# Filter taps on all partitions: a block transposition in place of fp32 matmuls in a convolution and ReGLU kernel

## The chip, the cores and the metric

The kernel runs on one core of one Trainium2 chip. The metric is the device time of one execution in microseconds (us); plain runs are timed without a profiler, and one more execution was profiled. TensorE is shown as PE (its weight loads as PEld), VectorE as DVE, ScalarE as ACT, GpSimd as POOL, SyncE as SP.

## What is computed

Eight sequences of 4096 tokens with 192 channels pass a causal convolution of seven taps and then a gated feed-forward layer. The taps are softmax weights, one set for each of eight heads of 24 channels.

```
w = weight - max(weight)              # weight: 8 heads x 7 taps
w = exp(w) / (sum(exp(w)) + 1e-9)
x_pad = 6 zero tokens ahead of x      # x: 8 x 4096 x 192
y[b, s, h, :] = sum over k of w[h, k] * x_pad[b, s + k, h, :]
out = (max(y @ w_gate, 0) * (y @ w_val)) @ w_out    # 192 -> 1536 -> 192
```

## The kernel before

The eight sequences are worked on in two streams of four, side by side: 64 rows of TensorE's array, and 64 channels of a third, belong to each stream. A unit is 1024 tokens of both streams; there are 16 units. For each unit and each half of 512 tokens, `gate_val` (L539) runs twelve column blocks of 128: six 64-row matmul pairs for gate and value (L552), a Relu on ACT (L563), a product on DVE (L564). `project` (L647) then multiplies by w_out (L581), copies out of PSUM (L607) and stores.

The convolution is done in two ways. For most of the kernel it is done off TensorE: POOL reads and rearranges x for a unit ahead (L203, L476), SP transposes it (L480), and ACT, DVE and POOL form the seven products and sums, with the taps as a scalar for each channel (`tap`, read at L496, L512, L526). The first unit can't wait for that. Its two blocks of 512 tokens are convolved on TensorE by `conv_dense` (L352): x stands as tokens by channels, and each head has a band matrix of 118 by 112 with its seven taps along the diagonals. Matmuls (L377) of 32 and fewer channels go to four column groups of the array, two for each stream.

The order of instructions on every engine is the order of the program text (the schedule is manual); the waits between engines are put in by the framework.

What is done ahead of the first convolution, with the names that matter:

- `wr` is the weight, 8 partitions by 7; it is loaded first on SP's queue (L101). Behind it on the same queue comes x of the first block, first stream, into a staging area in fp32 (L122), and the first 96 tokens of both streams (L138). The second stream comes through POOL's queue, cast on the way, into `x_h` (L127).
- `spaced` is a mask that POOL makes with a memset (L126) and an affine_select (L128). DVE sums it in two ways (`summed`, L238) to get `same` and `places`.
- DVE and ACT form the maximum (L251), the exponentials `ex`, each repeated 16 times (L254), the sum and its reciprocal (L258, L259). Two fp32 matmuls (L272, one instruction in the text) spread the taps from 8 partitions to 112. `diag` (L282) is taps times mask, and 14 matmuls (L292) build the bands in PSUM from `places` and `diag`; `fill_band` (L332) copies them to SBUF.
- `warm_up` (L154) gives TensorE matmuls whose result is not read: six and a half of 512 columns at the start, one behind L272, one behind L292.
- `taps` (L304) is the scaled taps on 8 partitions. Ten DMAs of SP (L310) spread them over `tap`, ahead of the first convolution; POOL copies `tap` to the other 64 partitions much later (L698).
- ACT casts the first stream's x in two pieces (L317), DVE the first tokens (L338).
- In `conv_dense`, for the first block and the first third of the channels, `both_halves` copies w_gate and w_val to the other 64 partitions (L177), and the matmuls run stream by stream:

```
        late = (1, 2, 3, 4, 0)
        both = [(jj, (0, 1)) for jj in late]
        if g == 0 and c == 0:
            both = [(jj, (st,)) for st in range(2) for jj in late[0:4]] + both[4:]
```

`first_block` (L387) does the three thirds and evicts each (L392) to `xc`, which L552 reads.

Of the kernel before, what the change touches and what calls it, by code (L numbers as in the profile page):

```python
# [7 lines left out]

FP = mybir.dt.float32
F16 = mybir.dt.float16  # L10
ACTF = mybir.ActivationFunctionType
ALU = mybir.AluOpType

# [2 lines left out]
def kernel(  # L16
# [12 lines left out]
    nc = tc.nc  # L29

    B, S, D = x.shape
    H, KW = weight.shape
    G = D // H
# [3 lines left out]
    NCH = D // 64  # L37
# [11 lines left out]
    UNIT = 2 * WIN  # L49
# [11 lines left out]
    const = ctx.enter_context(tc.tile_pool(name="const", bufs=1))  # L61
# [5 lines left out]
    xcpool = ctx.enter_context(tc.tile_pool(name="xcpool", bufs=3))  # L67
# [3 lines left out]
    psum = ctx.enter_context(tc.tile_pool(name="psum", bufs=4, space=bass.MemoryType.PSUM))  # L71
# [22 lines left out]

    xts = {}
    ROWS0 = DSUB + PAD
    GAP = 12
    SEG = 16
    NSEG = SUB // SEG
    wr = const.tile([H, KW], FP)  # L100
    nc.sync.dma_start(out=wr[:], in_=weight)  # L101
# [13 lines left out]
    def body(st):  # L115
# [4 lines left out]
        )  # L120

    nc.sync.dma_start(out=stage(0, SUB, 0, 1, 1, GSUB - 1), in_=body(0))  # L122
# [3 lines left out]
    nc.gpsimd.memset(spaced[:], 0.0)  # L126
    nc.gpsimd.dma_start(out=xts[0][0:SUB, 1:GSUB, 1, :], in_=body(1))  # L127
    nc.gpsimd.affine_select(  # L128
        out=spaced[:, :, GAP : GAP + SEG],
        in_=ones[0:SUB, 0 : KW * SEG].rearrange("p (k s) -> p k s", k=KW),  # L130
        pattern=[[-SEG, KW], [-1, SEG]],
        compare_op=ALU.is_equal,
        fill=0.0,
        base=0,
        channel_multiplier=1,
    )
    nc.vector.memset(stage(0, 32, 0, 2, 0, 1), 0.0)
    nc.sync.dma_start(  # L138
        out=stage(PAD, FIRST, 0, 2, 0, 1),
# [1 line left out]
            tensor=x.tensor, offset=x.offset, ap=[[D, FIRST], [NB * S * D, 2], [1, D]]  # L141
        ),
    )
    spare = const.tile([H, 1], FP)
    nc.scalar.activation(spare[:], ones[0:H, 0:1], ACTF.Exp)

    places = const.tile([SUB, 2 * SUB], F16)
    nc.vector.memset(places[:], 0.0)
# [3 lines left out]
    def warm_up(*widths):  # L152
        for n, w in enumerate(widths):
            nc.tensor.matmul(  # L154
                out=warm[:, n % 2, 0:w], lhsT=busy[:, 0:128], rhs=busy[:, 0:w], start=True, stop=True
            )

    warm_up(512, 512, 512, 512, 512, 512, 256)

# [69 lines left out]
    pool_halves(3)  # L229
    load_w(5, 2)  # L230

    ex = const.tile([H, KW + 1, SEG], FP)
    nc.vector.memset(ex[:], 1e-9)
    some = spaced[:, 0, 0:1]

    def summed(out, step, n, at):
        with nc.allow_low_precision("one of the terms is not zero"):
            nc.vector.tensor_reduce(  # L238
                out=out,
                in_=bass.AP(  # L240
                    tensor=some.tensor,
                    offset=some.offset + at,
                    ap=[some.ap[0], [1, n], [step, KW]],
                ),
                axis=mybir.AxisListType.X,
                op=ALU.add,
            )

    pitch_k = SEG + 2 * GAP
    mx = const.tile([H, 1], FP)  # L250
    nc.vector.tensor_reduce(  # L251
        out=mx[:], in_=wr[:], axis=mybir.AxisListType.X, op=ALU.max, negate=True
    )
    nc.scalar.activation(  # L254
        ex[:, 0:KW, :], wr[:].unsqueeze(2).to_broadcast([H, KW, SEG]), ACTF.Exp, bias=mx[:]
    )
    sm = const.tile([H, 1], FP)
    nc.vector.tensor_reduce(out=sm[:], in_=ex[:, :, 0], axis=mybir.AxisListType.X, op=ALU.add)  # L258
    nc.vector.reciprocal(sm[:], sm[:])  # L259
    over = const.tile([H, H], FP)  # L260
    nc.vector.tensor_scalar(
        out=over[:],
        in0=spaced[0:H, 0, GAP : GAP + H],
        scalar1=sm[:],
        scalar2=None,
        op0=ALU.mult,
    )
    same = const.tile([SUB, SEG], FP)
    summed(same[:], pitch_k, SEG, GAP)
    summed(places[:, SUB - SEG : SUB - SEG + SEG + KW - 1], pitch_k - 1, SEG + KW - 1, GAP)  # L270
    spread = psum.tile([128, 2, 512], FP, name="ps")
    nc.tensor.matmul(  # L272
        out=spread[0:SUB, 0, 0:H],
        lhsT=ex[:, 0:KW, :].rearrange("h k s -> h (k s)"),
        rhs=over[:],
        start=True,
        stop=True,
    )
    warm_up(512)
    diag = const.tile([SUB, H, SEG], F16)  # L280
    with nc.allow_low_precision("products with one and zero"):
        nc.vector.tensor_tensor(  # L282
            out=diag[:],
            in0=spread[0:SUB, 0, 0:H].unsqueeze(2).to_broadcast([SUB, H, SEG]),
            in1=same[:].unsqueeze(1).to_broadcast([SUB, H, SEG]),
            op=ALU.mult,
        )
    bps = psum.tile([128, 2, 512], FP, name="ps")
    HB = H // 2
    for a in range(2):  # L290
# [7 lines left out]
                skip_group_check=True,  # L298
            )

    warm_up(512)

    taps = const.tile([H, KW], FP)
    nc.scalar.activation(taps[:], ex[:, 0:KW, 0], ACTF.Copy, scale=sm[:])  # L304
    tap = const.tile([128, NCH, KW], FP)
    for h in range(H):
        r = G * h
        while r < G * (h + 1):
            c, n = r // 64, min(64 - r % 64, G * (h + 1) - r)
            nc.sync.dma_start(  # L310
                out=tap[r % 64 : r % 64 + n, c, :],
                in_=taps[h : h + 1, :].unsqueeze(1).to_broadcast([1, n, KW]),
            )
            r += n

    for cols in (slice(0, 64), slice(64, D)):
        nc.scalar.copy(  # L317
            out=xts[0][0:ROWS0, 1:GSUB, 0, cols],
            in_=stage(0, ROWS0, 0, 1, 1, GSUB - 1)[:, :, cols],
        )  # L320
    bands, wide_bands, ends = {}, {}, []

    def fill_band(a, heads, copy):
# [10 lines left out]
            in_=from_.rearrange("p (b h s) -> p h b s", h=HB, s=SEG)[:, lo : lo + n],  # L334
        )

    fill_band(0, [0, 1, 2], nc.vector.tensor_copy)
    nc.vector.tensor_copy(  # L338
        out=xts[0][0 : FIRST + PAD, 0, :, :], in_=stage(0, FIRST + PAD, 0, 2, 0, 1)
    )  # L340
    fill_band(0, [3], nc.vector.tensor_copy)
    fill_band(1, [4, 5], nc.scalar.copy)
    fill_band(1, [6, 7], nc.scalar.copy)

    def band(h):
# [2 lines left out]
    xc = {}  # L348
# [3 lines left out]
    def conv_dense(g, c, ps, bank):  # L352


        xt = xts[g]
        if g == 0 and c == 0:
            xc[0] = xcpool.tile([128, NCH, UNIT], F16, name="xc")
            both_halves(nc.vector.tensor_copy, 0, Wg)
            both_halves(nc.vector.tensor_copy, 0, Wv)
        toks = GROUPS[g][1]  # L360
        t0 = toks[0]
        ends = toks[1:] + [t0 + WIN]
        late = (1, 2, 3, 4, 0)
        both = [(jj, (0, 1)) for jj in late]
        if g == 0 and c == 0:
            both = [(jj, (st,)) for st in range(2) for jj in late[0:4]] + both[4:]
        for jj, sts in both:
            col, n = toks[jj] - t0, ends[jj] - toks[jj]
            rows = n + PAD
            for second in range(2):  # L370
                for st in sts:
                    for k2 in range(2):
                        k = 2 * c + k2
                        h0, h1 = 32 * k // G, (32 * k + 31) // G
                        h, m = (h0, G * h1 - 32 * k) if second else (h1, 32)
                        p0 = 64 * st + 32 * k2
                        nc.tensor.matmul(  # L377
                            out=ps[p0 : p0 + m, bank, col : col + n],
                            lhsT=xt[0:rows, jj, st, 32 * k : 32 * k + m],
                            rhs=band(h)[0:rows, 0:n],  # L380
                            start=True,
                            stop=True,
                            tile_position=(0, p0),
                            skip_group_check=True,
                        )

    def first_block():  # L387
        for c in range(NCH):
# [300 lines left out]


    first_block()
    both_halves(nc.vector.tensor_copy, 1, Wg)
    both_halves(nc.vector.tensor_copy, 1, Wv)
    pool_halves(4)
# [74 lines left out]
```

## Time and profile before

| | |
|---|---|
| plain runs | 765.69 us median of 3 (765.66 to 765.76) |
| the profiled execution | 767.53 us |
| its span, first to last instruction | 765.8 us |
| granted TensorE clock, mean of the span | 1.000 |
| busy PE, PEld | 762.0 us, 547.1 us |
| busy DVE, ACT, POOL | 705.9 us, 601.1 us, 378.9 us |

A row of the timeline gives start and length in us, the engine (with a q for its queue, where it issues a DMA), the line, the operation, the tile written and those read, shapes, how many instructions the row merges, and in brackets how long the engine was idle before it and what ended that. A row of the chain gives start, length, and what ran. A row of a table of windows gives the window, its length, and for each engine the busy time and the number of instructions that touch it; then the granted clock, the load of the DMA engines and GB/s. A row of DMA issues ends with the median time from issue to landing.

### The profile page before, as it was taken

Reading aid. Unit: us, or ns where it says so; the run is one execution under the profiler, and the core shown is the slowest. Engines: PE = TensorE matmul, PEld = TensorE weight load, DVE = VectorE, ACT = ScalarE, POOL = GpSimd, SP = SyncE. Lnnn points to the kernel's source line nnn. Section 1 sums busy time; section 2 is a strip of 40 time slices with the busy share of each in tenths; the row PEclk is TensorE's granted clock in tenths of the full one; section 3 lists DMA queues with packets and bytes.
Section 4 is the critical chain, followed back from the end, with each engine's and each line's share of the span. In section 5 each row is a group of like instructions: output and inputs, shape, how many; then the busy total and the mean of one; then the engine's idle time right before and its main releaser. Section 6 shows DMA issues by size and latency. Waiting matters only on the chain.

```text
span 765.8 us, 25125 instructions
## 1 busy us (share of the span) xinstructions
PE 762.0 (99%) x10937; PEld 547.1 (71%) x10937; DVE 705.9 (92%) x763; ACT 601.1 (78%) x735; POOL 378.9 (49%) x248
## 2 busy tenths in 40 slices
PE   9999999999999999999999999999999999999998
PEld 5496785957759577695866858668595775957758
DVE  6998999999999999999999999999999999999891
ACT  6787887878878787887878878788787887876571
POOL 8518549093570926719165290853908447090000
PEclk9999999999999999999999999999999999999999
DMA  9969138180362904529063281732818034110202
GB/s 121 125 111 138 18 95 82 53 117 11 99 79 66 114 23 99 56 85 94 23 109 50 85 93 44 110 25 89 89 44 130 8 96 61 65 49 13 73 1 84
DMA packets 131830, 56.00 MB, mean 73 GB/s; under 512 B 96392, under 2 KB 131720, under 8 KB 131720
## 3 DMA queue, kind: packets, MB, share of 16 engines
q1 hardware_dynamic: 90680, 38.81, 23.2%
q0 software_dynamic: 40896, 15.50, 20.3%
q8 instruction: 85, 1.39, 0.8%
q14 instruction: 25, 0.20, 0.1%
q10 hardware_dynamic: 144, 0.10, 0.0%
HBM read 31.48 MB, written 25.17 MB: 74 GB/s over the span
## 4 chain that ended last, share of the span: by engine, by line
PE 100%; ACT 0%; issue 0%
PE ps L552 65%; PE ps L581 32%; PE ps L630 1%; PE ps L377 1%; PE ps L154 1%; PE ps L292 0%; PE ps L415 0%; PE ps L272 0%; ACT acc L607 0%
## 5 line engine op out<-in xcount | busy, mean ns | idle before, releaser
L564 DVE TENSOR_TENSOR hT<-gr,ps 128x1024 f16<-128x1024 f16 (+1 forms) x386 | 468.9, 1215 | 36.9 <-ACT gr L563 9.8
L563 ACT ACTIVATE gr<-ps 128x1024 f16<-128x1024 f32 (+1 forms) x386 | 393.2, 1020 | 102.2 <-PE ps L552 100.0
L502 POOL TENSOR_TENSOR prods<-prods 128x1344 f32<-128x1344 f32 x70 | 212.5, 3035 | 289.6 <-DVE prods L498 286.2
L552 PE MATMUL ps<-xc,Wg 64*128 64x512 f16 x2304 | 322.3, 376 | 0.0
L552 PE MATMUL ps<-xc,Wv 64*128 64x512 f16 x2304 | 322.3, 376 | 0.0
L581 PE MATMUL ps<-Wo,hT 64*128 64x192 f16 x5952 | 249.1, 243 | 0.0
L581 PEld LDWEIGHTS <-hT 64*128 64x128 f16 x5952 | 247.0, 94 | 2.9
L552 PEld LDWEIGHTS <-Wv 64*128 64x128 f16 x2304 | 143.5, 94 | 105.3 <-issue 0.6
L552 PEld LDWEIGHTS <-Wg 64*128 64x128 f16 x2304 | 142.3, 94 | 103.1 <-issue 0.6
L526 DVE SCALAR_TENSOR_TENSOR acc<-x_r,tap,acc 128x576 f32<-128x576 f16 x225 | 165.3, 811 | 0.0
L496 ACT ACTIVATE prods<-x_r,tap 128x448 f32<-128x448 f16 x222 | 130.1, 660 | 0.0
L607 ACT COPY out_s<-ps 128x768 f32<-128x768 f32 (+1 forms) x64 | 45.6, 712 | 51.1 <-PE ps L581 39.8
L203 POOL DMA_DIRECT2D x_e<-in_x_dram x58 | 47.0, 823 | 16.0 <-ACT acc L512 12.3
L476 POOL COPY x_p<-x_e 128x960 f16<-128x960 f16 (+1 forms) x58 | 50.4, 907 | 1.7 <-DMA x_e<-in_x_dram 1.6
L502 POOL TENSOR_TENSOR xc<-prods 128x1344 f16<-128x1344 f32 x14 | 42.4, 3028 | 1.1
L526 DVE SCALAR_TENSOR_TENSOR xc<-x_r,tap,acc 128x576 f16<-128x576 f16 x45 | 34.0, 811 | 0.0
L512 ACT ACTIVATE acc<-x_r,tap 128x576 f32<-128x576 f16 x45 | 31.5, 766 | 0.0
L498 DVE TENSOR_SCALAR prods<-x_r,tap 128x448 f32<-128x448 f16 x70 | 26.6, 449 | 0.0
L607 DVE COPY out_s<-ps 128x384 f32<-128x384 f32 (+1 forms) x16 | 8.6, 540 | 11.5 <-PE ps L630 9.4
L630 PE MATMUL ps<-Wo,hT 128*128 128x192 f16 x96 | 8.1, 246 | 0.0
L630 PEld LDWEIGHTS <-hT 128*128 128x128 f16 x96 | 7.9, 98 | 0.2 <-issue 0.2
L377 PEld LDWEIGHTS <-x_h 110*32 110x32 f16 (+7 forms) x240 | 4.4, 107 | 0.9 <-ACT x_h L317 0.5
(55 smaller groups left out, 60.2 us busy)
## 6 DMA issues: line engine op xcount, KB each, us to landing
out_dram<-out_s SPq DMA_DIRECT2D x62, 384.0 KB, 2.8
x_e<-in_x_dram POOLq DMA_DIRECT2D x34, 192.0 KB, 7.1
x_e<-in_x_dram POOLq DMA_DIRECT2D x24, 240.0 KB, 5.3
x_r<-x_p SPq DMA_TRANSPOSE x131, 5.0
Wo<-in_moe_w_out_dram POOLq DMA_DIRECT2D x1, 576.0 KB, 7.2
x_h<-in_x_dram POOLq DMA_DIRECT2D x2, 210.0 KB, 6.0
Wg<-in_moe_w_gate_dram POOLq DMA_DIRECT2D x4, 96.0 KB, 4.4
Wv<-in_moe_w_val_dram POOLq DMA_DIRECT2D x4, 96.0 KB, 4.0
```

What stands on the lines that cost most here:

```text
L203: first = nc.gpsimd.dma_start(out=xe[:, j0 + start : j0 + n, st, :, :].rearrange("p j c r -> p j (c r)"), in_=bass.AP(tensor=x.tensor, off ...
L476: nc.gpsimd.tensor_copy(out=xp[:, j0 : j0 + n, :, st, :], in_=xe[:, j0 : j0 + n, st, :, :])
L496: engine.activation(out=out, in_=in_, func=ACTF.Copy, scale=scale)
L498: engine.tensor_scalar(out=out, in0=in_, scalar1=scale, scalar2=None, op0=ALU.mult)
L502: nc.gpsimd.tensor_tensor(out=pr[:, 0] if k < KW - 1 else xc[v + 1][:, :, LDVE:UNIT], in0=pr[:, 0], in1=pr[:, k], op=ALU.add,)
L512: nc.scalar.activation(out=accs[v][:, c, :], in_=shifted(v, c, 0, 0), func=ACTF.Copy, scale=tap[:, c, 0:1],)
L526: nc.vector.scalar_tensor_tensor(out=xc[v][:, c, 0:LDVE] if k == KW - 1 else acc[:, c, :], in0=shifted(v, c, k, 0), scalar=tap[:, c, k : k ...
L552: nc.tensor.matmul(out=pss[i][:, st, :], lhsT=W[64 * st : 64 * st + 64, c, 128 * f : 128 * (f + 1)], rhs=xcb[64 * st : 64 * st + 64, c, WI ...
L563: nc.scalar.activation(out=gr[:, sts], in_=pss[0][:, sts], func=ACTF.Relu)
L564: nc.vector.tensor_tensor(out=h[:, f, sts], in0=gr[:, sts], in1=pss[1][:, sts], op=ALU.mult)
L581: mm = nc.tensor.matmul(out=outs[q], lhsT=h[64 * r : 64 * r + 64, f, st, 128 * q : 128 * (q + 1)], rhs=Wo[64 * r : 64 * r + 64, f, :], sta ...
L607: one(out=dst[:, step * j : step * j + step], in_=src[:, step * j : step * j + step])
```

## The change

Every step between the weight and the bands is made anew, and some steps are moved.

- The weight is loaded 16 times over, to 128 partitions, by ACT's queue; SP's queue begins with x.
- POOL makes one iota (`steps`) in place of memset and affine_select. From it DVE works out the masks: two shifts with a mask for the token and the tap of a row, one more for a column's number, an addition and two comparisons.
- Maximum, subtraction, Exp, sum and reciprocal run on 128 partitions. Each group of 32 partitions keeps two of the seven taps (`mine`), repeats each 16 times in a second Exp (`wide`), scales them (`even`), and a transposition of 32x32 blocks on DVE gives each of 112 partitions (tap, token) its eight heads (`turned`), which `diag` reads in place of PSUM. The two fp32 matmuls are gone.
- The spare activation ahead of the weights is gone.
- Warm-up: seven and a half matmuls of 512 columns at the start, none before L292, half a one behind it.
- The first stream's cast is in three pieces of 64 channels, with ACT's two band copies between them; DVE copies the band of head 3 before it casts the first tokens.
- The first convolution runs both streams side by side from its first matmuls on; the copies of w_gate and w_val stand ahead of it as before.
- `taps` and its ten DMAs come behind the first block.

```diff
-    wr = const.tile([H, KW], FP)
-    nc.sync.dma_start(out=wr[:], in_=weight)
+    wr = const.tile([128, KW], FP)
+    nc.scalar.dma_start(
+        out=wr[:], in_=bass.AP(tensor=weight.tensor, offset=weight.offset, ap=[[0, 128 // H], [KW, H], [1, KW]])
+    )
...
-    ones = const.tile([128, SUB], FP)
-    nc.vector.memset(ones[:], 1.0)
-    spaced = const.tile([SUB, KW, SEG + 2 * GAP], FP)
-    nc.gpsimd.memset(spaced[:], 0.0)
+    steps = const.tile([SUB, 64], I32)
+    nc.gpsimd.iota(steps[:], pattern=[[1, 64]], base=0, channel_multiplier=64)
     nc.gpsimd.dma_start(out=xts[0][0:SUB, 1:GSUB, 1, :], in_=body(1))
-    nc.gpsimd.affine_select(
...
-    warm_up(512, 512, 512, 512, 512, 512, 256)
+    warm_up(512, 512, 512, 512, 512, 512, 512, 256)
...
+    s_of = bits(steps[:, 0:1], 1, 6, SEG - 1)
+    k_of = bits(steps[:, 0:1], 1, 10, 7)
+    col = bits(steps[:, 0:NROW], NROW, 0, 63)
+    r_of = const.tile([SUB, 1], FP)
+    nc.vector.tensor_tensor(out=r_of[:], in0=s_of[:], in1=k_of[:], op=ALU.add)
+    same = const.tile([SUB, SEG], FP)
+    nc.vector.tensor_tensor(
+        out=same[:], in0=col[:, 0:SEG], in1=s_of[:].to_broadcast([SUB, SEG]), op=ALU.is_equal
+    )
+        nc.vector.tensor_scalar(
+            out=places[:, SUB - SEG : SUB - SEG + NROW],
...
+    low = const.tile([128, KW], FP)
+    nc.vector.tensor_scalar(out=low[:], in0=wr[:], scalar1=mx[:], scalar2=None, op0=ALU.add)
+    nc.scalar.activation(ex[:, 0:KW], low[:], ACTF.Exp)
+    mine = const.tile([128, 2], FP)
+    for q in range(4):
+        rows = slice(32 * q, 32 * q + 32)
+        one = low[rows, 2 * q : min(2 * q + 2, KW)]
+        nc.vector.tensor_copy(out=mine[rows, :], in_=one if q < 3 else one.to_broadcast([32, 2]))
+    wide = const.tile([128, 2, SEG], FP, name="wide")
+    nc.scalar.activation(wide[:], mine[:].unsqueeze(2).to_broadcast([128, 2, SEG]), ACTF.Exp)
...
-    nc.tensor.matmul(
-        out=spread[0:SUB, 0, 0:H],
-        lhsT=ex[:, 0:KW, :].rearrange("h k s -> h (k s)"),
-        rhs=over[:],
...
-    warm_up(512)
+    turned = const.tile([128, 2 * SEG], FP)
+    nc.vector.transpose(out=turned[:], in_=even[:])
...
-            in0=spread[0:SUB, 0, 0:H].unsqueeze(2).to_broadcast([SUB, H, SEG]),
+            in0=turned[0:SUB, 0:H].unsqueeze(2).to_broadcast([SUB, H, SEG]),
...
-    warm_up(512)
...
+    warm_up(256)
...
-        if g == 0 and c == 0:
-            both = [(jj, (st,)) for st in range(2) for jj in late[0:4]] + both[4:]
-        for jj, sts in both:
+        for jj in (1, 2, 3, 4, 0):
...
     first_block()
+    taps = const.tile([H, KW], FP)
+    nc.scalar.activation(taps[:], ex[0:H, 0:KW], ACTF.Copy, scale=sm[0:H])
+    tap = const.tile([128, NCH, KW], FP)
+    for h in range(H):
...
```

More of the change, by code (lines that the diff above doesn't have):

```diff
@@ L143 @@
     )
-    spare = const.tile([H, 1], FP)
-    nc.scalar.activation(spare[:], ones[0:H, 0:1], ACTF.Exp)
     places = const.tile([SUB, 2 * SUB], F16)
@@ L230, with bits @@
     load_w(5, 2)
[L232 to L250, printed above, removed]
+    ex = const.tile([128, KW + 1], FP)
+    nc.vector.memset(ex[:, KW : KW + 1], 1e-9)
+    def bits(src, n, down, keep):
+        out = const.tile([SUB, n], I32, name=f"bits{down}")
+        nc.vector.tensor_scalar(
+            out=out[:],
+            in0=src,
+            scalar1=down,
+            scalar2=keep,
+            op0=ALU.logical_shift_right,
+            op1=ALU.bitwise_and,
+        )
+        return out
+    NROW = SEG + KW - 1
+    s_of = bits(steps[:, 0:1], 1, 6, SEG - 1)
[6 more added lines that the diff above has]
+        out=same[:], in0=col[:, 0:SEG], in1=s_of[:].to_broadcast([SUB, SEG]), op=ALU.is_equal
+    )
+    with nc.allow_low_precision("zero and one"):
+        nc.vector.tensor_scalar(
+            out=places[:, SUB - SEG : SUB - SEG + NROW],
+            in0=col[:],
+            scalar1=r_of[:],
+            scalar2=None,
+            op0=ALU.is_equal,
+        )
+    mx = const.tile([128, 1], FP)
     nc.vector.tensor_reduce(
@@ L253 @@
     )
[L254 to L258, printed above, removed]
+    low = const.tile([128, KW], FP)
[8 more added lines that the diff above has]
+    nc.scalar.activation(wide[:], mine[:].unsqueeze(2).to_broadcast([128, 2, SEG]), ACTF.Exp)
+    sm = const.tile([128, 1], FP)
+    nc.vector.tensor_reduce(out=sm[:], in_=ex[:], axis=mybir.AxisListType.X, op=ALU.add)
     nc.vector.reciprocal(sm[:], sm[:])
-    over = const.tile([H, H], FP)
+    even = const.tile([128, 2 * SEG], FP)
     nc.vector.tensor_scalar(
-        out=over[:],
-        in0=spaced[0:H, 0, GAP : GAP + H],
+        out=even[:],
+        in0=wide[:].rearrange("p k s -> p (k s)"),
         scalar1=sm[:],
@@ L299 @@
             )
-    warm_up(512)
[L303 to L320, printed above, removed]
+    warm_up(256)
     bands, wide_bands, ends = {}, {}, []
@@ L335, in fill_band, with cast_third @@
         )
+    def cast_third(c):
+        cols = slice(64 * c, 64 * c + 64)
+        nc.scalar.copy(
+            out=xts[0][0:ROWS0, 1:GSUB, 0, cols],
+            in_=stage(0, ROWS0, 0, 1, 1, GSUB - 1)[:, :, cols],
+        )
     fill_band(0, [0, 1, 2], nc.vector.tensor_copy)
+    fill_band(0, [3], nc.vector.tensor_copy)
     nc.vector.tensor_copy(
@@ L370, in conv_dense @@
             for second in range(2):
-                for st in sts:
+                for st in range(2):
                     for k2 in range(2):
@@ L691 @@
     first_block()
+    taps = const.tile([H, KW], FP)
+    nc.scalar.activation(taps[:], ex[0:H, 0:KW], ACTF.Copy, scale=sm[0:H])
+    tap = const.tile([128, NCH, KW], FP)
+    for h in range(H):
+        r = G * h
+        while r < G * (h + 1):
+            c, n = r // 64, min(64 - r % 64, G * (h + 1) - r)
+            nc.sync.dma_start(
+                out=tap[r % 64 : r % 64 + n, c, :],
+                in_=taps[h : h + 1, :].unsqueeze(1).to_broadcast([1, n, KW]),
+            )
+            r += n
     both_halves(nc.vector.tensor_copy, 1, Wg)
```

31 lines of the change are left out of this document (8 added, 23 removed).

## The prediction

> **What bounds the kernel now.** I read the page first, then the chain of work that ended last, then the first 11 us of the timeline engine by engine, since nothing in the change touches code that runs later than that except the tap copies.
>
> The page gives the span and the clock that the profile says was granted:
>
> ```profile
> span 765.8 us, 25125 instructions
> ...
> PEclk9999999999999999999999999999999999999999
> ```
>
> The chain in order of time (start, length, what ran) is TensorE from one end to the other. Its first nine pieces are the part that the change rewrites, and what follows:
>
> ```profile
> 0.80 0.04 issue
> 0.85 2.93 PE ps L154 x7
> 3.78 0.47 PE ps L272 x2
> 4.25 0.54 PE ps L154
> 4.79 0.75 PE ps L292 x14
> 5.54 0.43 PE ps L154
> 5.96 3.15 PE ps L377 x68
> 9.11 7.10 PE ps L552 x57
> 16.21 1.48 PE ps L377 x120
> ```
>
> L154 is warm-up work whose result nobody reads, L272 the fp32 spreading matmuls, L292 the band building, L377 the convolution of the first block, L552 the gate and value matmuls. From 9.11 on TensorE has real work without a hole, so a start of L552 that is earlier or later by some amount moves the end of the kernel by about that amount. Before 9.11 only the last link counts: what lets the first convolution start, and how fast it runs.
>
> How fast it runs is not in the clock row, which says full speed throughout. It is in the starts of equal matmuls (64x512, two at a time):
>
> ```profile
> 9.44 0.63 PE L552 MATMUL ps<-xc,Wv 64*128 64x512 f16 x2
> 9.87 0.48 PE L552 MATMUL ps<-xc,Wg 64*128 64x512 f16 x2
> 10.19 0.38 PE L552 MATMUL ps<-xc,Wv 64*128 64x512 f16 x2
> 10.40 0.38 PE L552 MATMUL ps<-xc,Wg 64*128 64x512 f16 x2
> ```
>
> Pairs start 0.43 us apart, then 0.32, then 0.21. TensorE went from half pace to full pace at about 10.1 us. The chain says the same with the two convolutions of equal work: 3.15 us for the first, 1.48 for the second. So 1 us won before 10.1 us is worth 0.5 us at full pace, unless the moment of the switch moves as well. That moment is the largest unknown here.
>
> What lets the first convolution start? Three queues feed it:
>
> ```profile
> 0.81 0.40 SPq L101 DMA_DIRECT2D wr<-in_weight_dram  x1
> 1.27 0.34 SPq L122 DMA_DIRECT2D prods<-in_x_dram  x1
> 1.66 0.48 SPq L138 DMA_DIRECT2D prods<-in_x_dram  x1
> 3.54 7.73 SPq L310 DMA_DIRECT2D tap<-taps  x10
> ```
>
> ```profile
> 0.81 0.33 POOL L126 MEMSET spaced<- 112x280 f32 x1 [0.29 <-POOLq L753]
> 1.41 0.88 POOL L127 DMA_DIRECT2D x_h<-in_x_dram  x1 [0.27 <-issue]
> 2.38 0.36 POOL L128 TENSOR_SCALAR_AFFINE_SELECT spaced<-ones 112x112 f32<-112x112 f32 x1
> ```
>
> ```profile
> x_h<-in_x_dram POOLq DMA_DIRECT2D x1, 168.0 KB, 4.9
> ```
>
> The last row is the landing time of L127, the second stream's x: 1.41 + 4.9 = 6.3 us. The count of L377 matmuls per half microsecond (the x after PE busy) shows what that does:
>
> ```profile
> 5.85:6.35 0.50, 0.46 (x12) 0.46 (x14) 1.00 1.55 184
> 6.35:6.85 0.50, 0.50 (x26) 0.50 (x24) 1.00 1.51 184
> ```
>
> From 5.9 to 6.35 only one stream runs, 12 matmuls; from 6.35, with the second stream's x there, 26. The convolution uses four column groups of the array, two for each stream, and a stream's two groups need their own 2.6 us at half pace: 6.35 + 2.6 is the 9.0 at which it ends. The first stream's earlier start gained nothing. So the bound of this stage is the landing of L127 at 6.3, not the bands and not the taps.
>
> **The change part by part.** *Taps and bands.* Before, the taps' path on DVE and ACT is:
>
> ```profile
> 2.18 0.15 DVE L251 TENSOR_REDUCE mx<-wr 8x1 f32<-8x7 f32 x1 [0.46 <-DMA wr<-in_weight_dram]
> 2.78 0.15 DVE L258 TENSOR_REDUCE sm<-ex 8x1 f32<-8x8 f32 x1 [0.45 <-ACT ex L254]
> 2.96 0.15 DVE L259 RECIPROCAL sm<-sm 8x1 f32<-8x1 f32 x1
> 3.23 0.22 DVE L261 TENSOR_SCALAR over<-spaced,sm 8x8 f32<-8x8 f32 x1
> ...
> 4.29 0.29 DVE L282 TENSOR_TENSOR diag<-ps,same 112x128 f16<-112x128 f32 x1 [0.22 <-PE ps L272]
> 5.20 0.51 DVE L332 CAST band<-ps 128x336 f16<-128x336 f32 x1 [0.62 <-PE ps L292]
> ```
>
> ```profile
> 0.81 1.28 ACT L145 ACT_TABLE_LOAD   x1 [0.81 <-PEq L753]
> 2.10 0.20 ACT L145 ACTIVATE spare<-ones 8x1 f32<-8x1 f32 x1
> 2.36 0.39 ACT L254 ACTIVATE ex<-wr,mx 8x112 f32<-8x112 f32 x1
> 3.21 0.30 ACT L304 ACTIVATE taps<-ex,sm 8x7 f32<-8x7 f32 x1 [0.46 <-DVE sm L259]
> 4.88 0.92 ACT L317 CAST x_h<-prods 110x256 f16<-110x256 f32 x2 [1.37 <-DMA prods<-in_x_dram]
> ```
>
> The diagonal masks times taps (diag) are done at 4.29 + 0.29 = 4.58. The change removes the two fp32 matmuls (0.47), two mask reductions on DVE and the affine_select on POOL. It adds on DVE six mask operations ahead of the maximum, then the subtraction, four copies of 32 partitions, and the transposition. Weights land as before or a little later (the same issue at 0.81, but 128 rows of them): 2.2 to 2.5. The six mask operations wait for the iota, which no row shows; the nearest rows are POOL's memset at 0.33 and affine_select at 0.36, the ends are nothing and 0.7, twice those. I take 0.35, so they start at about 1.3 and at 0.18 each (the step from L258 to L259) end at 2.4. Then, by these rows: maximum at 2.5, subtraction 2.7, copies 4 x 0.15 to 3.5, the second Exp 0.39 to 3.9, the scaling 0.22 to 4.15, the transposition 0.2 (ends: 0.15 of L259 and 0.51 of L332; its 32 columns stand nearest to the small operations), diag 0.29 to 4.7. The first Exp, the sum and the reciprocal run beside the copies. The table load now follows the DMA issue on ACT, 0.81 + 0.40 + 1.28 = 2.5, just ahead of the first Exp at 2.9. So diag ends at 4.5 to 4.9, against 4.58: no gain, perhaps 0.1 of loss, and the work that covers it is L127's flight until 6.3. Bands then follow as before, 0.4 of L292 and 0.51 of cast: 5.7 to 6.1.
>
> [...]
>
> *x first on SyncE.* L122 moves from 1.27 to 0.81 and L138 with it, 0.46 earlier. The first stream is not the bound, so directly this is worth nothing. But its 336 KB leave the DMA engines 0.46 sooner, and L127's packets come behind them. Bounds for L127's landing: nothing gained, or the whole 0.46, with the iota's difference to the memset on top (0.33 sooner to 0.37 later). I take 0.25 earlier: 6.05.
>
> *Order of the convolution, casts and copies.* The first matmuls no longer run one stream ahead. By the counts above that start gained nothing, so it costs nothing as long as the second stream lands last. The casts on ACT, 0.92 in two parts, become three with the bands' copies between them; they waited for the first stream's landing until 4.88 and can begin at about 4.4, so the first two parts are done well before 6.0, and the third is read by the last third of the convolution alone.
>
> *Warm-up.* One more full warm-up ahead (0.85 + 7.5 x 0.43 = 4.1 instead of 3.78), one less behind, a half one left. TensorE then idles about 0.6 us before L292 and about 0.4 before the convolution, about 1 us together, where before it was covered but for some tenths.
>
> *Tap copies behind the first block.* The ten issues (7.73) move from 3.54 to behind the convolution's evictions, about 9.7 to 17.4. SP's next work comes at 29.80, and the reader is POOL:
>
> ```profile
> 24.53 0.25 POOL L698 COPY tap<-tap 64x21 f32<-64x21 f32 x1
> ```
>
> ```profile
> 29.80 12.67 SPq L480 DMA_TRANSPOSE x_r<-x_p  x9
> ```
>
> Even if the last of them needed as long as L127, 4.9, it would land at 17.4 + 4.9 = 22.3, 2.2 us ahead of the reader. Cost nothing.
>
> *The sum.* The convolution starts 0.25 to 0.3 earlier, L552 at 8.8 instead of 9.1. If the pace still doubles at 10.1, the head start was made at half pace and is worth 0.15. Profiled time: 767.53 (1.73 outside the span of 765.8); 767.53 - 0.15 = 767.4. The plain runs' median, 765.69, stands 1.84 below the profiled execution; the same 0.15 off it gives 765.5.
>
> **The rivals.** *Full pace comes later (slower).* The switch at 10.1 followed an almost unbroken stretch of TensorE work since 4.25 (the chain). With the two holes, that stretch would begin only with the convolution at 6.1, 1.85 later; the switch would come at 11.9, and 1.85 at half pace costs 0.9. Less 0.15: 766.4. If the pace is raised in steps and one is missed, the loss is larger: as long again as from the convolution's full load at 6.35 to the switch, 3.75 us, at half pace costs 1.9, less 0.15: 767.4. It decides as soon as the holes count as rest. [...]
>
> *Full pace comes sooner (faster).* If the longer first warm-up raises the pace before the convolution, that takes 1.48 as the second one does: L552 from about 7.7, and by 10.1 it has 2.4 us of full pace where before it had half of 1.0. Gain 1.9: 763.8. For it speaks the 3.2 us of unbroken warm-up; against it that 2.93 were not enough before.
>
> *Nothing moves.* L127 lands at 6.3 as before, since POOL's issue is as late: 765.7.
>
> *The second stream or the taps come late (slower).* An iota of 0.7 puts the convolution 0.35 later, worth 0.2 to 0.35; taps that land after 24.5 hold POOL's queue, with lane loads and the transpositions behind them. To cost 1.5 us this needs 4 us of lateness; 767.3.
>
> **How the numbers follow.** A measurement of this kernel can tell 0.2%, 1.5 us, from no change. Forecast and "nothing moves" together 0.48, later pace 0.28 (0.09 of it within the bound, 0.19 beyond), sooner pace 0.18, late x or taps 0.06. So faster 0.18, within 0.48 + 0.09 = 0.57, slower 0.19 + 0.06 = 0.25. The range reaches to the sooner pace at 763.8 and just past the missed step, to 767.5; the likeliest cases' own range is 765.0 to 766.0.
>
> **What would show it.** In the changed profile: x_h from POOL landing at 6.0 to 6.1 and the convolution's four groups starting together then; diag ending at 4.5 to 4.9; the first L552 at 8.7 to 8.9; pairs 0.43 apart until about 10.1 and 0.21 after; POOL's tap copy not waiting. It is wrong if 0.21 appears a microsecond or more sooner or later, if the bands and not x release the convolution, or if any hole opens in TensorE's chain after 17 us.

## The result and the profile after

The changed kernel takes 770.28 us in the median of 6 runs (769.14 to 772.28), the kernel before 765.74 (765.66 to 765.83) beside it: a ratio of 1.0063 [1.0047, 1.0079], 4.5 us slower, and 2.8 us above the top of the range. The profiled execution of the changed kernel took 769.36 us with a span of 767.6.

The chain of work of the kernel after that ended last, in order of time (start, length, what ran), begins with a DMA:

```profile
0.74 4.35 DMA wr<-in_weight_dram
...
5.12 0.17 DVE mx L256
...
7.40 0.30 DVE diag L284
...
7.75 0.91 PE ps L295 x14
...
8.88 2.48 PE ps L364 x118
11.36 6.61 PE ps L542 x60
...
19.45 24.74 PE ps L542 x228
```

Where TensorE had led the chain from 0.85 on, it now enters at 7.75. The weight load, the maximum that reads it, the steps from there to diag, the bands and the convolution follow one another without a gap. From 19.45 on nothing new happens. The same piece in the chain of before stands here:

```profile
17.68 24.73 PE ps L552 x228
```

It is 1.77 us earlier, and the spans of the two profiled executions differ by 1.8 (767.6 and 765.8). So the whole difference between these two executions arises in the first 12 us. Why the medians lie 4.5 us apart and not 1.8 is told under *From lateness to time* below.

The timeline of the kernel after (start, duration, engine, line, what; the idle time and its releaser in brackets):

```profile
0.74 0.66 ACTq L101 DMA_DIRECT2D wr<-in_weight_dram  x1
0.74 0.39 SPq L124 DMA_DIRECT2D prods<-in_x_dram  x1
0.84 0.17 POOL L126 IOTA steps<- 112x64 int32 x1 [0.40 <-POOLq L756]
1.42 0.89 POOL L127 DMA_DIRECT2D x_h<-in_x_dram  x1 [0.40 <-issue]
1.43 1.28 ACT L261 ACT_TABLE_LOAD   x1 [1.43 <-PEq L756]
5.12 0.16 DVE L256 TENSOR_REDUCE mx<-wr 128x1 f32<-128x7 f32 x1 [3.13 <-DMA wr<-in_weight_dram]
5.58 0.21 ACT L261 ACTIVATE ex<-low 128x7 f32<-128x7 f32 x1 [2.86 <-DVE low L260]
7.16 0.21 DVE L281 STREAM_TRANSPOSE turned<-even 128x32 f32<-128x32 f32 x1
7.75 0.91 PE L295 MATMUL ps<-diag,places 112*128 112x64 f16 x14 [3.61 <-DVE diag L284]
8.88 2.48 PE L364 MATMUL ps<-band,x_h 110*32 110x104 f16 x120
11.29 0.39 PE L542 MATMUL ps<-xc,Wg 64*128 64x512 f16 x2
```

The maximum starts at 5.12 instead of 2.18: the weights land 2.94 us later. L256 to the end of diag takes 5.12 to 7.69, 2.57 us, as against 2.40 before: the new chain from the maximum to diag is not what makes the start late. The second stream's x (L127) still takes 4.9 us from its issue:

```profile
x_h<-in_x_dram POOLq DMA_DIRECT2D x1, 168.0 KB, 4.9
```

It has landed at 1.42 + 4.9 = 6.32, some 2.5 us before the convolution starts. TensorE has meanwhile stood idle for 3.61 us.

The windows of the kernel after (from:to, length, then busy time and count of PE, PEld, DVE, ACT and POOL, the granted clock, DMA share, GB/s) show a second loss:

```profile
4.10:7.50 3.40, 0.04 (x1) 0.00 (x0) 2.02 (x11) 1.04 (x4) 3.40 (x6) 1.00 1.36 161
7.52:10.90 3.38, 3.14 (x112) 2.90 (x115) 2.69 (x7) 1.49 (x4) 3.33 (x6) 0.50 1.30 146
10.94:14.00 3.06, 3.06 (x61) 1.76 (x52) 2.31 (x5) 2.20 (x5) 2.26 (x4) 1.00 1.30 165
```

In the first window TensorE is busy 0.04 of 3.40 us. In the next, with TensorE 93% busy, the clock is 0.50, and from 10.94 on it is 1.00. The bands and the first convolution ran at half pace, behind the idle stretch: 0.91 and 2.48 us, where the experiment below that keeps TensorE busy has 0.57 and 1.64. What sets the moments at which the clock fell and rose, these rows do not show. The 1.00 of the first window alone can't be relied on, though: this kernel's warm-ups before 4.1 start 0.43 us apart, half the pace of the gate pairs' 0.21 to 0.23 from 11.29 on, and the column shows 1.00 there too.

### The profile page after: what moved, and what is told of

It is laid out like the page before. It is cut to its first block, busy times and chain, and to the rows that moved or that the text cites. A ratio compares the mean times of both kernels' runs of the same rounds, so it can differ in the third digit from the quotient of the medians.

```text
span 767.6 us, 25123 instructions
## 1 busy us (share of the span) xinstructions
PE 760.2 (99%) x10935; PEld 546.2 (71%) x10935; DVE 707.4 (92%) x772; ACT 601.6 (78%) x736; POOL 378.4 (49%) x247
## 4 chain that ended last, share of the span: by engine, by line
PE 99%; DMA 1%; DVE 0%; issue 0%; ACT 0%; DVEq 0%
PE ps L542 65%; PE ps L571 32%; PE ps L620 1%; DMA wr<-in_weight_dram 1%; PE ps L364 1%; PE ps L295 0%; DVE mine L266 0%; PE ps L405 0%; ACT acc L597 0%; DVE diag L284 0%; DVE even L273 0%; DVE low L260 0%; DVE turned L281 0%; PE ps L143 0%; DVE sm L271 0%
## 5 line engine op out<-in xcount | busy, mean ns | idle before, releaser
L542 PE MATMUL ps<-xc,Wv 64*128 64x512 f16 x2304 | 322.1, 376 | 0.0
L542 PE MATMUL ps<-xc,Wg 64*128 64x512 f16 x2304 | 322.1, 376 | 0.0
L542 PEld LDWEIGHTS <-Wv 64*128 64x128 f16 x2304 | 143.2, 94 | 105.2 <-DVE hT L554 0.3
L542 PEld LDWEIGHTS <-Wg 64*128 64x128 f16 x2304 | 142.5, 94 | 102.7
L143 PE MATMUL ps<-const-bfloat16-1.0 128*128 128x512 bf16 (+1 forms) x9 | 3.8, 579 | 0.8 <-PEq L756 0.8
```

The source lines that it names most:

```text
L542: nc.tensor.matmul(out=pss[i][:, st, :], lhsT=W[64 * st : 64 * st + 64, c, 128 * f : 128 * (f + 1)], rhs=xcb[64 * st : 64 * st + 64, c, WI ...
```

## The experiments

The theory after this profile: the load of 28 bytes to each of 128 partitions lands late, and TensorE's idle time costs its pace on top. Rivals for the late landing were x's 336 KB ahead of it, ACT's queue, and the number of rows. Rivals for the time were the pace alone, the tap copies, and the order of the convolution. The kernel before stood beside every set: 765.77 (14 runs), 765.92 (33) and 765.78 (24).

### Where the weight load loses its time

**The load first on SP's queue, ahead of x.**

```diff
     wr = const.tile([128, KW], FP)
-    nc.scalar.dma_start(
+    nc.sync.dma_start(
...
```

> The changed kernel with the weight's load (all 128 partitions) first on SyncE's queue again and x behind it. Theory 'behind x': the weight lands late because x's packets are ahead of it; with x behind it lands at 2.2 to 2.7 us instead of 5.1, diag ends at about 5.0 instead of 7.7, the convolution starts at about 6.3 when the second stream's x has landed, and the time falls to 765.5 to 767.0. Theory 'ACT's queue': the same, since it is SyncE's queue now. Theory '128 short rows': it still lands at 4 us or later, diag stays behind 6.5 and the time above 768.5. The hole in TensorE's work shrinks from 3.6 us to about 0.9; if such a hole still costs pace, the time lies up to 1.7 above that of the kernel before, and scatters.

768.88 us, ratio 1.0046 [1.0031, 1.006]. Its timeline:

```profile
0.74 0.72 SPq L101 DMA_DIRECT2D wr<-in_weight_dram  x1
4.14 0.16 DVE L256 TENSOR_REDUCE mx<-wr 128x1 f32<-128x7 f32 x1 [2.15 <-DMA wr<-in_weight_dram]
```

The maximum starts at 4.14, 0.98 sooner than in the kernel after and still 1.96 later than before. With nothing ahead of it the load is late all the same.

**The load on ACT's queue, x held back until it is issued.**

```diff
-    nc.sync.dma_start(out=stage(0, SUB, 0, 1, 1, GSUB - 1), in_=body(0))
-    nc.vector.memset(stage(0, 32, 0, 2, 0, 1), 0.0)
+    blank = nc.vector.memset(stage(0, 32, 0, 2, 0, 1), 0.0)
+    x_first = nc.sync.dma_start(out=stage(0, SUB, 0, 1, 1, GSUB - 1), in_=body(0))
+    tc.add_manual_dep(x_first.ins, blank.ins.name, SYNC, reason="behind the weight")
```

> The changed kernel with the weight still on ACT's queue, but x's first load held on SyncE's queue until DVE's first memset is through (about 1.3 us), so that the weight is issued first. Theory 'behind x': the weight lands at 2.2 to 2.8 and diag ends near 5.0, as in the kernel with the weight first on SyncE's queue; time 765.5 to 767.5. Theory 'ACT's queue': it lands at 4 to 5 as in the changed kernel, time near 770. Theory '128 short rows': 4 or later too.

768.85 us, 1.0041 [1.0026, 1.0056]; x issues at 1.28, and in the timeline:

```profile
4.38 0.16 DVE L257 TENSOR_REDUCE mx<-wr 128x1 f32<-128x7 f32 x1 [2.40 <-DMA wr<-in_weight_dram]
```

Within 0.24 us of SP's queue with the weights first: ACT's queue is not the cause.

**The kernel before with x first and its 8 rows of weights on ACT's queue.**

```diff
-    nc.sync.dma_start(out=wr[:], in_=weight)
+    nc.scalar.dma_start(out=wr[:], in_=weight)
```

> The kernel before with one edit: the weight (8 partitions, 8 short rows) goes on ACT's queue and x is first on SyncE's. Theory 'behind x': the weight lands at 3.2 to 5 us instead of 2.2, the first fp32 matmul and diag move back by as much, and the time rises by 1 to 4 us to 767 to 770. Theory 'ACT's queue': the same. Theory '128 short rows': 8 rows land at about 2.2 to 2.5 as before, and the time stays at 765.7 or falls a little.

766.65 us, 1.0012 [1.0002, 1.0021]. Its timeline:

```profile
2.19 0.15 DVE L251 TENSOR_REDUCE mx<-wr 8x1 f32<-8x7 f32 x1 [0.48 <-DMA wr<-in_weight_dram]
2.84 0.37 ACT L254 ACTIVATE ex<-wr,mx 8x112 f32<-8x112 f32 x1
```

Eight rows land at 2.19 beside x as they did without it (2.18). What this order costs comes from ACT: the table load now stands behind the DMA issue (1.43 instead of 0.81), Exp starts at 2.84 instead of 2.36, and diag ends 0.35 later (4.93). Five of its ten runs lie at 765.9 to 766.2, five at 767.1 to 767.6. x first did not delay eight rows.

**128 rows without the repetition.** The load of the first experiment, 28 bytes to each partition, from 128 different rows of x (768 bytes apart) instead of the weights sixteen times over; its taps are other numbers.

```diff
-    out=wr[:], in_=bass.AP(tensor=weight.tensor, offset=weight.offset, ap=[[0, 128 // H], [KW, H], [1, KW]])
+    out=wr[:], in_=bass.AP(tensor=x.tensor, offset=x.offset + 8192 * D, ap=[[D, 128], [1, KW]])
```

> The kernel with the weight's load first on SyncE's queue, but its 128 rows of 28 bytes are read from 128 different rows of x in place of 16 times the same 8 rows of the weight; so the taps are made of other numbers. Theory 'same bytes': reading the same 224 bytes 16 times is what made the load land at 4.1 us; apart, it lands at 2.2 to 2.8, diag ends at 5.0 to 5.3 and the time is 766 to 767.5. Theory 'row count': 128 short rows cost 2 us wherever they are; it lands at 3.8 to 4.4 and the time stays at 768.5 to 769.2.

766.21 us, 1.0005 [0.9996, 1.0014]. Its timeline:

```profile
0.74 0.39 SPq L101 DMA_DIRECT2D wr<-in_x_dram  x1
2.33 0.16 DVE L256 TENSOR_REDUCE mx<-wr 128x1 f32<-128x7 f32 x1 [0.35 <-DMA wr<-in_x_dram]
```

Same bytes, same partitions, same queue: 2.33 instead of 4.14, and the issue takes 0.39 instead of 0.72. Neither 128 rows nor 28 bytes a row was slow here; the load that reads the same 224 bytes sixteen times was.

**The repetition, with its eight rows 768 bytes apart in x,** and **the same three dimensions without repetition.** Both on SP's queue ahead of x.

```diff
-    out=wr[:], in_=bass.AP(tensor=weight.tensor, offset=weight.offset, ap=[[0, 128 // H], [KW, H], [1, KW]])
+    out=wr[:], in_=bass.AP(tensor=x.tensor, offset=x.offset + 8192 * D, ap=[[0, 128 // H], [D, H], [1, KW]])
```

and in the second kernel

```diff
+    out=wr[:], in_=bass.AP(tensor=x.tensor, offset=x.offset + 8192 * D, ap=[[H * D, 128 // H], [D, H], [1, KW]])
```

> As the kernel with rows apart (load first on SyncE's queue, numbers of x in place of the weight), but the 128 rows are 16 times the same 8 rows of x, which lie 768 bytes apart. Theory 'repetition': it is reading the same bytes again that is slow; the load lands at 3.8 to 4.4 us, the time is 768.5 to 769.5. Theory 'closeness': it was that all rows lie in one piece of 224 bytes; 8 rows over 5 KB land at 2.2 to 3.0. Theory 'pattern': the repeat written as a dimension of its own is slow for the queue that makes the packets; 3.8 to 4.4 as well.

> The same load, written with the same three dimensions of 16, 8 and 7, but the 16 groups step on through x, so that no row is read twice. Theory 'repetition' or 'closeness': it lands at 2.2 to 2.5 us as with rows apart, and the time is 765.9 to 767.5. Theory 'pattern': 3.8 to 4.4, and 768.5 or more.

Repeated: 767.97 us, 1.0028 [1.0015, 1.0041].

```profile
0.74 0.72 SPq L101 DMA_DIRECT2D wr<-in_x_dram  x1
2.95 0.16 DVE L256 TENSOR_REDUCE mx<-wr 128x1 f32<-128x7 f32 x1 [0.96 <-DMA wr<-in_x_dram]
```

Not repeated: 767.30 us, 1.0014 [1.0004, 1.0024].

```profile
2.33 0.16 DVE L256 TENSOR_REDUCE mx<-wr 128x1 f32<-128x7 f32 x1 [0.35 <-DMA wr<-in_x_dram]
```

The number of dimensions cost nothing (2.33 again). The repeated source cost 0.62, half of it in the issue (0.72 instead of 0.38): 2.95 is in the range of the theory 'closeness', not of 'repetition'. The remaining 1.19, from 2.95 to the first experiment's 4.14, came when the repeated rows also lay within 224 bytes, in the weight and not in x. The weight read once, by 8 rows, landed at 2.18. Whether closeness alone would do it for 128 rows, without repetition, was not tried. The median of the kernel without repetition is 1.1 us above that of the straight 128 rows, with the weights as early in both profiles; its runs lie at 765.8 and at 767.3 to 767.7, most likely the step between an early and a late full pace that comes up again below.

**128 different rows behind x.** The kernel after, on ACT's queue, with the source of the 128 different rows.

> The changed kernel's order, x first on SyncE's queue and the 128-row load on ACT's, but the rows are read from 128 different rows of x. It prices x ahead of the load without the repetition. Theory 'x ahead costs 1 us': the load lands 0.9 to 1.1 later than the 2.3 of rows apart ahead of x, at 3.2 to 3.4, and the time is 767 to 768.5. Theory 'x ahead costs only with slow rows': it lands at 2.3 to 2.6, the time is 765.9 to 767.5 as with rows apart.

769.05 us, 1.004 [1.0027, 1.0052]. Its timeline:

```profile
3.71 0.16 DVE L256 TENSOR_REDUCE mx<-wr 128x1 f32<-128x7 f32 x1 [1.73 <-DMA wr<-in_x_dram]
```

x, issued at the same 0.74 from SP's queue, costs these rows 3.71 - 2.33 = 1.38, though they go through ACT's queue; that is more than either theory gave. The 8 rows of weights on ACT's queue, with x as far ahead, landed at 2.19 and showed no such cost.

So the 2.94 us of lateness, in the order in which the kernels add up: 0.15 for 128 rows instead of 8 (2.18 to 2.33), 0.62 for repetition, 1.19 for repetition within 224 bytes, 0.98 for x ahead (of which 0.24 or less may be ACT's queue, by the experiment that held x back). Each landing is that of one profiled execution. The same load in two kernels started its reader at 5.12 and 5.08, at 2.31 and 2.23, and twice at 2.33, so the three large steps are clear, and the 0.15 is not by much.

### What the lateness costs, and what the pace

**The kernel after with TensorE kept busy until the masks are ready.**

```diff
-    warm_up(512, 512, 512, 512, 512, 512, 512, 256)
+    warm_up(*[512] * 16, 256)
```

> The changed kernel with nine more warm-up matmuls of 512 columns ahead of the bands, so that TensorE has work from 0.8 us until the bands' matmuls at 7.7; the late weight stays. Theory 'pace': the hole of 3.6 us in TensorE's work is what keeps it at half pace through the first convolution in some executions and longer in others; filled, the convolution takes 1.4 to 1.5 us instead of 2.5, the first gate matmul starts at 10.1 to 10.3 instead of 11.3, the runs lie within 0.5 us of each other, and the time is 767.7 to 768.5, that is 2.0 to 2.7 above the kernel before, the late weight's own part. Theory 'late start alone': the pace is not set by the hole; the time stays at 769 to 772.

769.15 us (768.52 to 769.24), 1.0041 [1.0026, 1.0056]. Its timeline on TensorE, DVE and POOL:

```profile
8.71 1.64 PE L364 MATMUL ps<-band,x_h 110*32 110x104 f16 x120 [0.28 <-ACT band L317]
...
8.98 0.82 POOL L166 COPY Wg<-Wg 64x768 f16<-64x768 f16 x1
9.15 0.80 DVE L166 COPY Wg<-Wg 64x384 f16<-64x384 f16 x1
...
9.75 0.82 POOL L166 COPY Wv<-Wv 64x768 f16<-64x768 f16 x1
9.87 0.84 DVE L166 COPY Wv<-Wv 64x384 f16<-64x384 f16 x1
10.28 0.39 PE L542 MATMUL ps<-xc,Wg 64*128 64x512 f16 x2
...
10.74 0.69 DVE L382 CAST xc<-ps 128x512 f16<-128x512 f32 x1
...
11.48 0.39 PE L542 MATMUL ps<-xc,Wg 64*128 64x512 f16 x2 [0.33 <-DVE xc L382]
```

The last seven warm-ups take 2.23 us from 5.00 on, more than seven at 0.21 (1.5) and less than seven at 0.43 (3.0); by an estimate from these numbers the pace is full from about 6.3 on. The bands then take 0.57 instead of 0.91, and the convolution takes 1.64 instead of 2.48. The scatter of the runs shrinks from 3.1 us (six runs) to 0.7 (four), and the median by 1.1. That is what the theory 'pace' said of the convolution and the scatter, nearly, but its 767.7 to 768.5 came out too low. L542 starts at 10.28, 1.01 sooner than in the kernel after, but most of that is lost again: DVE's two weight copies hold back the eviction on which the third pair of L542 waits, and that pair starts at 11.48, against 11.73. The 0.25 between these two is the difference of the two profiled executions (769.12 and 769.36). The other 3.4 us of the median stay. The experiment with the late taps, further down, has the third pair at

```profile
8.36 0.38 PE L539 MATMUL ps<-xc,Wg 64*128 64x512 f16 x2
```

and the first at 7.91. So 10.28 - 7.91 = 2.37 us of them are the late start and 0.75 more, to 11.48 - 8.36 = 3.12, the wait for the eviction, by these two profiles.

**The kernel after with 8 rows of weights loaded on SP's queue, the other 120 cleared by POOL.**

```diff
-    nc.scalar.dma_start(
-        out=wr[:], in_=bass.AP(tensor=weight.tensor, offset=weight.offset, ap=[[0, 128 // H], [KW, H], [1, KW]])
-    )
+    nc.gpsimd.memset(wr[:], 0.0)
+    nc.sync.dma_start(out=wr[0:H, :], in_=weight)
```

> The changed kernel with the weight on 8 partitions alone, first on SyncE's queue; the other 120 partitions hold zeros, so 15 of 16 copies of the taps are left out of the computation, and every other step is the change's. It prices the rest of the change with an early weight. The weight lands at 2.4 to 2.6 (it waits for a memset first), diag ends at 4.8 to 5.1, the bands let the convolution start at 6.0 to 6.3, about when the second stream's x lands. Theory 'the weight alone': the time is 765.5 to 766.3, no different from the kernel before beyond 0.5 us. Theory 'pace': the holes of about 0.8 and 0.4 us, which the kernel before covers, cost up to 1.7 us in part of the executions; the median is 766.5 to 767.5 and the runs scatter by over 1 us. Theory 'something else is lost' (the order of DVE's work, the taps' late copies): above 767.5 in every run.

767.27 us (765.80 to 767.46), 1.0014 [1.0005, 1.0024]. Its timeline:

```profile
2.31 0.16 DVE L255 TENSOR_REDUCE mx<-wr 128x1 f32<-128x7 f32 x1 [0.33 <-DMA wr<-in_weight_dram]
4.97 0.91 PE L294 MATMUL ps<-diag,places 112*128 112x64 f16 x14 [0.83 <-DVE diag L283]
6.11 2.57 PE L363 MATMUL ps<-band,x_h 110*32 110x104 f16 x120
```

This is the change as the prediction had it: diag ends at 4.92, just past its 4.5 to 4.9, and the convolution starts at 6.11. It takes 2.57 us behind a hole of 0.83.

**The same with the holes filled.**

```diff
-    warm_up(512, 512, 512, 512, 512, 512, 512, 256)
+    warm_up(*[512] * 9, 256)
...
-    warm_up(256)
+    warm_up(512, 256)
```

> The kernel with the weight on 8 partitions (15 of 16 copies of the taps left out) and, on top, the holes in TensorE's work filled: two more warm-up matmuls of 512 columns ahead of the bands, one more behind them. Theory 'pace': the 767.3 of that kernel is its holes; filled, the median falls to 765.7 to 766.2, the kernel before's, with at most a few executions above 767. Theory 'no pace': it stays at 767.0 to 767.5.

765.86 us (765.65 to 766.32), 0.9999 [0.999, 1.0009]. Its chain, in order of time:

```profile
0.78 4.21 PE ps L142 x10
4.99 0.89 PE ps L294 x14
5.89 0.45 PE ps L142 x2
6.33 1.48 PE ps L363 x120
7.81 6.61 PE ps L541 x60
```

TensorE is unbroken, the convolution runs in 1.48, and the time is that of before. With an early load and no hole the whole rest of the change costs nothing and wins nothing. The holes alone were worth 767.27 - 765.86 = 1.41 us in the median, or 1.27 when each is taken against the kernel before beside it (765.92 and 765.78). That is no fixed price. The kernel with 128 different rows on SP's queue has a hole as long (1.00 ahead of the bands), and 7 of its 10 runs took 766.3 or less, its median 0.3 above that of before; with eight rows and the holes it was 2 of 10. In the profiled executions the bands took 0.57 behind the first kernel's hole and 0.91 behind the second's. Runs above 766.5 were 3 of 10 and 8 of 10 with these holes, none of 10 with them filled. That such runs met the late pace is an estimate, since only one run of each kernel has a trace. No version beat the kernel before.

### The other steps

**The kernel before with POOL's DMA of the second stream ahead of its memset.**

```diff
-    nc.gpsimd.memset(spaced[:], 0.0)
     nc.gpsimd.dma_start(out=xts[0][0:SUB, 1:GSUB, 1, :], in_=body(1))
+    nc.gpsimd.memset(spaced[:], 0.0)
```

> The kernel before with one edit: POOL issues the second stream's x ahead of its memset instead of behind it. The landing that releases the convolution's second pair of column groups moves from 6.3 to about 5.7; then the bands at 5.9 bound it. Theory 'the landing binds': 0.3 to 0.45 us are won, 765.3 to 765.5, outside the spread of the kernel before (765.6 to 766.1). Theory 'hidden': the convolution ends when it did, 765.6 to 765.9.

766.06 us, 1.0006 [0.9997, 1.0015]. Its timeline:

```profile
1.40 0.88 POOL L126 DMA_DIRECT2D x_h<-in_x_dram  x1 [0.88 <-POOLq L753]
6.34 1.54 PE L377 MATMUL ps<-band,x_h 110*32 110x104 f16 x104 [0.35 <-DMA x_h<-in_x_dram]
```

With nothing ahead of it the DMA still starts at 1.40, after 0.88 of idle time. What stands on POOL before it had cost nothing, so taking it away could win nothing. The second row confirms that this landing releases the second stream's matmuls.

**The kernel before with the taps and their ten DMAs behind the first block,** the code of the change's last part.

```diff
-    taps = const.tile([H, KW], FP)
-    nc.scalar.activation(taps[:], ex[:, 0:KW, 0], ACTF.Copy, scale=sm[:])
...
     first_block()
+    taps = const.tile([H, KW], FP)
+    nc.scalar.activation(taps[:], ex[:, 0:KW, 0], ACTF.Copy, scale=sm[:])
...
```

> The kernel before with one edit: the scaled taps and their ten copies on SyncE's queue come behind the first block, as in the change. Theory 'costs nothing': POOL's reader at 24.5 us finds them landed, 765.6 to 766.0; with fewer small packets ahead of it the second stream's x may land 0.1 sooner. Theory 'taps late': POOL waits for them by 1 to 2 us, the lane's transpositions slide, and a hole opens in TensorE's work near 59 us: 766.5 to 768.

766.07 us, 1.0003 [0.9992, 1.0014]. Its timeline (span 764.2):

```profile
5.90 2.09 PE L364 MATMUL ps<-band,x_h 110*32 110x104 f16 x120
7.91 0.39 PE L539 MATMUL ps<-xc,Wg 64*128 64x512 f16 x2
8.83 7.81 SPq L686 DMA_DIRECT2D tap<-taps  x10
23.86 0.25 POOL L698 COPY tap<-tap 64x21 f32<-64x21 f32 x1
```

The move costs nothing by itself; POOL does not wait. One of its ten runs took 770.09, the others at most 766.15; no trace shows what that one met. The row of L539 matters more: in this execution the gate matmuls start at 7.91, where the profiled execution of before had 9.04 (9.11 in its chain).

## Why the prediction was wrong

**The step that failed** is "Weights land as before or a little later (the same issue at 0.81, but 128 rows of them): 2.2 to 2.5". The term was sized at 0 to 0.3 us and measured 2.94. It was taken from the old load's row, of another access pattern, with no bound from above, although no row showed a load of this form. The profile of before had slower loads in the same stage: 4.9 us, as L127 takes from its issue, would have bounded it at 0.81 + 4.9 = 5.7, and the 5.1 measured lies inside. In the 0.15 between 8 and 128 rows the step was right; it overlooked that the source repeats, and that the same part of the change puts x ahead.

**What followed from it.** The cover that it counted on, "the work that covers it is L127's flight until 6.3", was worth a few tenths: by the prediction's own sum bands were ready at 5.7 to 6.1. With 2.9 of lateness the bands became the bound, which the prediction named as the sign of its failure. It gave this no price and no chance among the rivals; "the taps come late" there meant the tap copies.

**From lateness to time.** The right thing to compare the profile with is the ordinary execution of before, as the experiment with the late taps shows it: 7.91 and a span of 764.2. After, 11.29 and 767.6: 3.38 later at L542, 3.4 longer. Of it 2.98 is the later start of the convolution (5.90 to 8.88), the rest that convolution's slower pace. The median of after lies another 0.92 above its profiled execution (770.28 - 769.36). That no profile shows; since it went away with the scatter when TensorE was kept busy (769.15), it is most likely the pace; at what moments that changed in the unprofiled runs, no run shows.

**The profiled execution and the median.** The prediction kept 1.84 us as a constant offset between them. Most likely it was no offset: of 71 runs of before beside the experiments, 66 lie between 765.6 and 766.3 and 5 between 767.4 and 767.7, and the profiled one, with 767.53 and full pace only at 10.1, belongs with the five. The profiles of the other kernels go the same way: with the first gate pair still 0.61 us long at 9.30 and 8.93 (0.39 at full pace), x first took 767.6 and the three dimensions without repetition 767.58; with full pace before the first gate matmuls at 7.9 and 7.8 (0.39 long), the late taps took 766.08 and the filled eight rows 765.93. Why an execution of before reaches full pace late, although the profiled one shows no hole of TensorE from 0.85 on, no run here shows. By this reading "if the pace still doubles at 10.1" described an uncommon case, and what *Full pace comes sooner* describes, priced at 763.8, most runs of before already do: with full pace in the convolution from 6.33 on (1.48 us) and no holes the last experiment on the pace took 765.86.

**The rival *Full pace comes later*** was borne out in part: with eight rows and the holes the convolution took 2.57, filled 1.48, but with 128 different rows the bands ran in 0.57 behind a hole of 1.00. That holes count as rest was the author's estimate, and so was the missed step of 3.75 us; no run shows such a step. For the holes it spoke of, about 1 us together, it asked 0.9 to 1.9, and 1.41 was measured between the two kernels with eight rows; in the kernel with 128 different rows a hole as long cost 0.3 in the median. In the changed kernel the hole is 3.61, and this came on top of the late start instead of in its place. *Nothing moves* is what is left once load and holes are mended.

**The smaller terms.** The iota took 0.17 (0.35 was taken), the transposition 0.21 (0.2). The four copies took 0.80 (0.6). The table load took 1.28 (1.43 to 2.71), and Exp waited for DVE's subtraction long after it, until 5.58. L127 landed at 6.3, not 6.05: its issue at 1.42 did not move with what precedes it, and x's issue at 0.74 instead of 1.27 did not shorten its 4.9 us to landing. The tap copies were "cost nothing" alone; in the kernel after they issue from 12.21 on, and the reader does wait:

```profile
25.69 0.20 POOL L701 COPY tap<-tap 64x21 f32<-64x21 f32 x1 [2.16 <-DMA tap<-taps]
```

No hole opens in TensorE's chain for it, so the 2.16 us stay on POOL. That sign of the prediction failed, without a cost that these profiles show.

## What to carry to other kernels

Price a changed load by its access pattern as well as its bytes (the same 3.5 KB landed at 2.33 and at 4.14): with no row of the same form, bound it by the slowest load of the same stage, and compare that with the few tenths by which the next wait covers it. A wait that leaves TensorE idle can cost twice, once for the time (here 2.98 us of later start) and once for the pace of what comes after (2.48 us of convolution against 1.64 with TensorE kept busy), so fill it or count both, the second as a chance and not as a fixed price. Before subtracting from a profiled execution, see whether it is an ordinary one: a gap between its time and the runs' median may come from the very stage under study.

## What was not expected of the hardware

- Reading 224 bytes of HBM sixteen times into 128 partitions landed at 4.14, the same amount from 128 rows 768 bytes apart at 2.33; the issue alone took 0.72 instead of 0.39.
- POOL's first DMA started at 1.40 to 1.46 in every trace, whether a memset, an iota or nothing stood ahead of it.
- DVE's copies of 64x384 took 0.80 and 0.84 us while POOL copied too, in the kernel after with TensorE kept busy. With the load early and the holes filled, where POOL issued DMAs meanwhile, the same two took 0.42 and 0.34. The two slow ones ended 0.15 and 0.14 us after the POOL copy beside them (9.95 and 9.80, 10.71 and 10.57). What made them slow is not shown: the overlap was not taken away by itself.
- The granted clock showed 1.00 from 4.97 to 8.32 in the kernel with eight rows and the holes, although its first convolution took 2.57 us from 6.11 on, against 1.48 filled: read the pace at the start of a kernel from equal matmuls.
